# Turning the attention's scores on VectorE instead of TensorE from block 3 on, in an attention and two-MoE kernel

## Chip, cores and metric

The kernel runs on one core of a Trainium2 chip. Times are device microseconds (us) of one execution; the time of the kernel is the median of three runs.

## The reference

Three stages over 4 x 768 = 3072 tokens of width 512, all in float32. `a` is chunked attention with 8 heads, `moe` a two-layer SiLU MLP, and `moe2` a soft mixture of 8 experts with 4 slots each.

```python
for c in range(nc):                       # chunks of 32 queries
    k_ctx = k[:, :, max(0, 32*c - 16):min(S, 32*c + 40)]      # 16 keys left, 8 right
    k_full = concatenate([mem_k, k_ctx]); v_full = concatenate([mem_v, v_ctx])   # 8 more: 64 keys
    a = exp(scale * q_c @ k_full.T - max); a = a / (sum(a) + 1e-09)
    out[:, :, 32*c:32*c + 32] = a @ v_full
x = out as [3072, 512]
h = x @ w_in; x = (h * sigmoid(h)) @ w_out            # 512 -> 2048 -> 512
logits = x @ phi                                       # 32 slots
d = softmax of logits over the tokens; slot_input = d.T @ x
slot_out[e] = relu(slot_input[e] @ w1[e]) @ w2[e]
out = (softmax of logits over the slots) @ slot_out
```

## The kernel before

The tokens go through in seven blocks (256, 384, 512, 512, 512, 512, 384). Blocks 0 and 1 run in an opening whose order is written out as a string; from block 2 on two nested loops run: over the blocks j, and in each over 16 slots i, one for each 128 columns of the hidden layer.

In a slot `emit_h` (L359) issues 12 matmuls that fill one PSUM bank with 128 hidden values of the block's tokens (ps_h; x and w_in are split into a high and a low part, and three products are added). Two banks take turns, 0 and 1, so the emission of slot i+2 may begin only when slot i's bank has been read. ScalarE reads it for `g_tanh` (L379), VectorE for `g_mult` (L383), and then `g_turn` (L387) turns the result in 32x32 squares on VectorE. `logits` (L402) multiplies four slots' results with a folded w_out and phi; it stands in three slots of a block, and for the last four in slot 0 of the next.

Beside that the slots hold two kinds of other work, put in by `at(j, i, half, ...)`: half 0 comes behind the emission (and the logits), half 1 behind tanh, mult and turn of the slot. The first kind is the attention of the tokens that the next block needs, in groups of 128 tokens. A group passes through three visits of `place`, which lie three slots apart (slots 1, 5, 8, 11, 14 of block 2, slots 5, 8, 11, 14 of blocks 3 to 5):

- its scores: TensorE in half 0 (`a_scores`, L266, queries in the partitions, 8 heads x 64 keys along a row); in half 1 max (L274, L278 at the ends of a sequence) and subtraction (L287, L290) on VectorE and exp (L293) on ScalarE, and a slot later sum, inverse (L297 to L301) and the product with it (L191) on POOL
- its turn: `a_turn` (L311) makes four TensorE transposes of 128x128 with the identity into one PSUM bank, `a_keep` copies it to SBUF on ScalarE; two heads' 64 keys then lie in the partitions
- its values: `a_values` (L326), 32 matmuls with 64x64 weights from v and 64x32 scores; `a_hi` on ScalarE and `a_lo` (L343) on VectorE split the result into the high and low part of x

So one slot holds values(g), turn(g+1) and scores(g+2), in this order on TensorE. The second kind of other work is the routing of the block before (`routing`, slots 0 to 9): softmax pieces on VectorE and ScalarE, `route_slots` (L504) on TensorE, and the sums `route_acc` (L515) on VectorE. The conversion of w_out (`wo_conv`: two ScalarE instructions and L214 on VectorE) is spread over slots by the list WO.

Each engine works its queue in program order; TensorE loads weights ahead. The unnormalized scores of all groups from 5 on lie in one place (A in aarena), and so did their turned form.

Of the kernel before, what the change touches and what calls it, by code (L numbers as in the profile page):

```python
# [7 lines left out]
F32 = mybir.dt.float32  # L8
# [5 lines left out]
ALU = mybir.AluOpType  # L14
# [7 lines left out]
NG = NTOK // 128  # L22
# [30 lines left out]
def attn_moe_softmoe_kernel(  # L53
# [13 lines left out]
    nc = tc.nc  # L67
# [116 lines left out]
    def copy(eng, out, in_):  # L184
        if eng == "a":
            nc.scalar.activation(out=out, in_=in_, func=ACTF.Copy)  # L186
        else:
            nc.vector.tensor_copy(out=out, in_=in_)
# [126 lines left out]
        copy(eng, at_t[g], ps_t.pop(g))  # L315

    def a_values(g, *bs):
        AT, vt = at_t.pop(g), v_t.pop(g)
        px = ps_t[g] = [bank(b, [128, 2, 128], "ps_x") for b in bs or (None, None)]
        for c in range(4):  # L320
            q = slice(32 * c, 32 * c + 32)
            for u in range(2):
                for s, r in ((0, 0), (1, 1), (0, 1), (1, 0)):
                    k, h = slice(64 * s, 64 * s + 64), slice(64 * r, 64 * r + 64)
                    n = 2 * r + u
                    nc.tensor.matmul(px[s][h, u, q], vt[k, n, c], AT[k, n, q], start=True, stop=True)  # L326

    def x_half(x, g, s):
        o = 128 * g - tok0[blk[g]]
        t = x[blk[g]][s]  # L330
        return bass.AP(tensor=t.tensor, offset=t[:, o:o + 1].offset, ap=[t.ap[0], [BLOCKS[blk[g]], 2], [1, 128]])
# [14 lines left out]

# [234 lines left out]

    slots = {}

    def at(j, i, half, fn, *args):
        slots.setdefault((j, i, half), []).append((fn, args))


    def place(j, i, values, turn, scores, b=None):  # L590
        if values is not None:
            at(j, i, 0, a_values, values)
            at(j, i, 0, load_v, values + 1)
            at(j, i, 1, a_hi, values)
            at(j, i, 1, a_lo, values)
        if turn is not None and turn < NG:
            at(j, i, 0, a_turn, turn, b)
            at(j, i, 1, a_keep, turn, "a")
        if scores is not None and scores < NG:
            at(j, i, 0, a_scores, scores)  # L600
            at(j, i, 0, load_qk, scores + 1)
            at(j, i, 1, a_max, scores)
# [25 lines left out]
    for j in range(3, NB):  # L628
        at(j, 0, 0, logits, j - 1, f_order(j - 1)[-1] // 4)
        routing(j, 0, j - 1)  # L630
    for n, i in enumerate((1, 5, 8, 11, 14)):
        g = tok0[3] // 128 - 1 + n
        place(2, i, g if n else None, g + 1, g + 2, (None, 2, 3, 3, 3)[n])
    for j in range(3, L):
        for n, i in enumerate((5, 8, 11, 14)[:BLOCKS[j + 1] // 128]):
            g = tok0[j + 1] // 128 + n
            place(j, i, g, g + 1, g + 2, 2 + (j + 1) % 2)
    at(3, 1, 0, load_ew, *words(garena, 3072, 4096))
    at(L, 4, 1, load_ew, *words(z, NF * BLOCKS[L], 10240))
    at(3, 6, 1, wp_copies)  # L640
    WO = [(2, 15)] + [(j, i) for j in range(3, L) for i in (2, 7, 10, 13, 15)]
    for u in range(16):
        for k in range(4):
            at(*WO[u], 1, wo_conv, u, k)
# [267 lines left out]
def _layout(inputs):  # L912
    import numpy as np

    f = np.float32
    c = np.ascontiguousarray
    q, k, vv = inputs["q"], inputs["k"], inputs["v"]
    mk, mv = inputs["mem_k"], inputs["mem_v"]
    B, H, S, D = q.shape
    G = S // 128  # L920

    blocks = [0, 1, 2, 3, 4, 5, 6, 19, 7, 8, 9, 10, 19, 11, 12, 13, 14, 19, 15, 16, 17, 18]
    starts = (0, 4, 9, 14)
    keys = np.zeros((2, B, H, G, 20, 8, D), f)
    for i, (src, mem) in enumerate(((k, mk), (vv, mv))):
        for g in range(G):
            lo, hi = max(0, 128 * g - 16), min(S, 128 * g + 136)
            rows = keys[i, :, :, g].reshape(B, H, 160, D)
            rows[:, :, lo - 128 * g + 16:hi - 128 * g + 16] = src[:, :, lo:hi]
            rows[:, :, 152:160] = mem  # L930
            keys[i, :, :, g] = rows.reshape(B, H, 20, 8, D)
    kk = keys[0][:, :, :, blocks].reshape(B, 4, 2, G, 176, D)
    qk = np.zeros((2, D, B, G, 4, 304), f)
    qk[..., 0:128] = q.reshape(B, 4, 2, G, 128, D).transpose(2, 5, 0, 3, 1, 4)
    qk[..., 128:304] = kk.transpose(2, 5, 0, 3, 1, 4)

    vw = np.stack([keys[1][:, :, :, blocks[n:n + 8]].reshape(B, 2, 2, 2, G, 64, D) for n in starts], axis=5)
    vw = vw.transpose(2, 6, 0, 4, 3, 1, 5, 7)
    w_in, w_out = inputs["moe_w_in"], inputs["moe_w_out"]
    win = w_in.reshape(4, 128, 16, 128).transpose(2, 1, 0, 3)  # L940

    woutt = w_out.reshape(16, 128, 4, 128).transpose(0, 3, 2, 1)
    wout = w_out.reshape(4, 4, 4, 32, 512).transpose(2, 0, 1, 3, 4)
    phi = inputs["moe2_phi"].reshape(4, 128, 32).transpose(1, 0, 2)
    w1 = inputs["moe2_w1"].reshape(2, 4, 4, 128, 2, 512).transpose(0, 2, 4, 3, 1, 5)
    w1 = c(w1).reshape(16, 128, 2, 1024).transpose(0, 2, 1, 3)

# [40 lines left out]
```

## Time and profile before

| | us |
|---|---|
| median of three runs (482.71 to 483.04) | 482.81 |
| the profiled execution, its own time | 482.95 |
| its span on the core | 481.2 |
| TensorE busy (matmuls) | 457.8 |
| VectorE busy | 310.0 |
| ScalarE busy | 194.5 |
| POOL busy | 41.8 |

The span is what the profile covers; the time of an execution is 1.75 us longer. Busy time is the time in which an engine works on an instruction; waits of a queue are not in it. Matmuls overlap in the records, so TensorE's busy time counts each stretch once. The chain that ended last is followed back from the last instruction, at each step to what released it; an engine that fills the chain is the one that sets the end there.

### The profile page before, as it was taken

The page shows a single profiled execution, that of the slowest core. Times are in us where ns is not written, and L with a number is a line of the kernel's source. Part 1 is how long each engine was busy: PE and PEld are TensorE (multiplying, and loading weights), DVE is VectorE, ACT ScalarE, POOL GpSimd, SP SyncE. Part 2 cuts the span into 40 slices and gives each one's busy share as a digit, 9 for nine tenths or more (in the row PEclk, how much of TensorE's full clock was granted, in tenths as well). Part 3 has the DMA queues.
Part 4 walks back from the last instruction along what each step waited for, and adds up shares of the span by engine and source line. Part 5 has one row for each costly group of instructions (what it writes and reads, how often), then busy time and mean ns, then how long its engine had stood idle before and what let it go on. Part 6 is the DMA issues. An engine that isn't in the chain of part 4 may idle for free.

```text
span 481.2 us, 14612 instructions
## 1 busy us (share of the span) xinstructions
PE 457.8 (95%) x6432; PEld 346.3 (72%) x6433; DVE 310.0 (64%) x687; ACT 194.5 (40%) x403; POOL 41.8 (9%) x41
## 2 busy tenths in 40 slices
PE   5889999999999999999999999999999999999981
PEld 2789888988776777677866778766787789543641
DVE  4837787787577766677867667686755765531061
ACT  3648788863342234234443244441433222311041
POOL 0412133210000001000110000010000000000000
PEclk9559999999999999999999999999999999999996
DMA  8937688564121235123442235411133997799998
GB/s 329 378 142 265 231 288 307 172 229 142 53 57 42 97 98 184 45 97 140 142 150 80 79 108 190 143 46 49 50 125 112 389 409 273 291 412 410 407 349 276
DMA packets 29727, 93.67 MB, mean 195 GB/s; under 512 B 2784, under 2 KB 9184, under 8 KB 29664
## 3 DMA queue, kind: packets, MB, share of 16 engines
q1 hardware_dynamic: 29664, 92.74, 53.0%
q8 instruction: 50, 0.82, 0.7%
q14 instruction: 13, 0.11, 0.1%
HBM read 86.44 MB, written 6.29 MB: 193 GB/s over the span
## 4 chain that ended last, share of the span: by engine, by line
PE 89%; DMA 4%; DVE 2%; ACT 1%; issue 1%; SPq 0%; DVEq 0%; ACTq 0%
PE ps_h L359 55%; PE ps_x L326 6%; PE ps_a L504 6%; PE ps_l L402 5%; PE ps_s L266 3%; PE ps_t L311 3%; PE ps_o L825 3%; PE ps_e L793 3%; DMA oarena<-in_woutt_dram 3%; DMA oarena<-in_win_dram 1%; PE ps_f L875 1%; PE ps_q L235 1%; PE ps_in L760 1%; PE ps_sum L741 1%; PE ps_r L419 1%
## 5 line engine op out<-in xcount | busy, mean ns | idle before, releaser
L359 PE MATMUL ps_h<-x,w 128*128 128x512 f32 (+2 forms) x704 | 152.5, 361 | 1.7 <-DVE garena L383 1.4
L359 PEld LDWEIGHTS ps_h<-x,w 128*128 128x128 f32 x704 | 125.2, 190 | 22.7 <-issue 5.0
L359 PE MATMUL ps_h<-x1a,w 128*128 128x512 f32 (+2 forms) x544 | 139.4, 363 | 0.0
L383 DVE SCALAR_TENSOR_TENSOR garena<-garena,ps_h 128x512 f32<-128x512 f32 (+2 forms) x112 | 67.9, 607 | 72.0 <-ACT garena L379 71.5
L359 PEld LDWEIGHTS ps_h<-x1a,w 128*128 128x128 f32 x544 | 99.6, 189 | 20.1 <-issue 6.1
L379 ACT ACTIVATE garena<-ps_h 128x512 f32<-128x512 f32 (+2 forms) x112 | 59.8, 534 | 132.9 <-PE ps_h L359 124.0
L387 DVE STREAM_TRANSPOSE z<-garena 128x512 f32<-128x512 f32 (+2 forms) x112 | 70.1, 631 | 4.5 <-PE ps_a L504 0.9
L191 POOL TENSOR_TENSOR aarena<-aarena,smm 128x512 f32<-128x512 f32 x19 | 20.6, 1085 | 233.9 <-DVE smm L301 204.6
L214 DVE SCALAR_TENSOR_TENSOR oarena<-oarena 128x512 uint32<-128x512 uint32 x46 | 32.6, 723 | 10.6 <-ACT oarena L208 10.4
L206 ACT ACTIVATE oarena<-oarena 128x512 f32<-128x512 f32 x46 | 30.5, 668 | 18.4 <-DMA oarena<-in_win_dram 11.7
L208 ACT ACTIVATE oarena<-oarena 128x512 uint32<-128x512 uint16 x48 | 31.7, 671 | 0.0
L326 PEld LDWEIGHTS ps_x<-aarena 64*64 64x64 f32 x1280 | 21.7, 139 | 12.5 <-issue 4.0
L504 PE MATMUL ps_a<-z,d 32*32 32x512 f32 x768 | 27.0, 598 | 0.6 <-DVE d L475 0.6
L326 PE MATMUL ps_x<-aarena 64*64 64x32 f32 x1280 | 24.1, 224 | 1.2 <-issue 1.2
L359 PE MATMUL ps_h<-x1b,w 128*128 128x512 f32 x64 | 25.0, 391 | 0.0
L293 ACT ACTIVATE aarena<-aarena 128x512 f32<-128x512 f32 x20 | 12.6, 631 | 30.5 <-DVE aarena L287 15.7
L402 PE MATMUL ps_l<-garena,aarena 128*32 128x512 f32 (+2 forms) x216 | 24.7, 544 | 0.0
L274 DVE TENSOR_REDUCE mx<-ps_s 128x4 f32<-128x256 f32 x48 | 17.8, 413 | 5.8 <-PE ps_s L266 5.8
L191 POOL TENSOR_TENSOR w<-oarena,w 128x512 fp32r<-128x512 f32 x12 | 15.8, 1319 | 55.4 <-ACT w L186 55.4
L504 PEld LDWEIGHTS ps_a<-z,d 32*32 32x32 f32 x768 | 12.1, 103 | 11.7 <-issue 7.0
L515 DVE SCALAR_TENSOR_TENSOR acc<-acc,al,ps_a 128x512 f32<-128x512 f32 x20 | 13.9, 743 | 7.0 <-PE ps_a L504 7.0
L266 PE MATMUL ps_s<-aarena 64*32 64x64 f32 x1280 | 17.2, 224 | 0.7 <-DMA aarena<-in_qk_dram 0.7
(194 smaller groups left out, 432.1 us busy)
## 6 DMA issues: line engine op xcount, KB each, us to landing
aarena<-in_qk_dram SPq DMA_DIRECT2D x20, 608.0 KB, 5.4
aarena<-in_v_dram SPq DMA_DIRECT2D x20, 512.0 KB, 4.3
w<-in_w_dram SPq DMA_DIRECT2D x20, 512.0 KB, 7.1
oarena<-in_win_dram SPq DMA_DIRECT2D x16, 512.0 KB, 5.6
oarena<-in_woutt_dram SPq DMA_DIRECT2D x16, 512.0 KB, 6.0
oarena<-in_wout_dram SPq DMA_DIRECT2D x16, 512.0 KB, 3.2
z<-in_w_dram SPq DMA_DIRECT2D x10, 512.0 KB, 7.8
oarena<-in_w_dram SPq DMA_DIRECT2D x9, 512.0 KB, 10.2
```

The costliest lines, as they stand in the source:

```text
L191: (nc.gpsimd if eng == "p" else nc.vector).tensor_tensor(**kw)
L206: nc.scalar.activation(out=x, in_=hi_w.bitcast(F32), func=ACTF.Prelu, scale=REBIAS, alpha=-(2.0**32))
L208: nc.scalar.activation(out=lo_w, in_=raw.bitcast(U16)[:, :, 1], func=ACTF.Copy, scale=2.0**-13, bias=-4095.75 / 8192)
L214: nc.vector.scalar_tensor_tensor(out=xb, in0=xb, scalar=3, in1=lo_w, op0=ALU.logical_shift_left, op1=ALU.bitwise_or)
L266: nc.tensor.matmul(ps[r][q, p], t[h, p, q], t[h, p, w:w + 64], start=True, stop=True)
L326: nc.tensor.matmul(px[s][h, u, q], vt[k, n, c], AT[k, n, q], start=True, stop=True)
L359: nc.tensor.matmul(ph, w_t[f][:, wi, 128 * c:128 * c + 128], x[c], start=(c == 0 and m == 0), stop=(c == 3 and m == 2),)
L379: nc.scalar.activation(out=g_tile(j, f), in_=h_t[j, f], func=ACTF.Tanh, scale=0.5)
L383: nc.vector.scalar_tensor_tensor(out=g, in0=g, scalar=1.0, in1=h_t.pop((j, f)), op0=ALU.add, op1=ALU.mult)
L387: nc.vector.transpose(out=z_view(j)[:, slot], in_=g_t[j, f])
L402: nc.tensor.matmul(rt[j, "pl"][32 * m:32 * m + 32], wp[:, f], g_t[j, f], start=(k == ks[0]), stop=(k == ks[-1] or j == L and m > 1 and k = ...
L504: nc.tensor.matmul(ps[q][32 * cg:32 * cg + 32], d[p, t], zv[p, :, t], start=(b < 4), stop=(b >= nb - 4), tile_position=(32 * q, 32 * cg),)
```

## The change

For groups 9 to 23 (the tokens of blocks 3 to 6) `a_turn` and `a_keep` are gone. `v_turn` takes their place on VectorE: one instruction turns all of A, 128 partitions by 512, in 32x32 squares, which puts the first or second 32 keys of each of the four chunks into the chunk's own 32 partitions; four instructions of 32 partitions by 256 turn the other 32 keys of a chunk and write them to the neighbouring 32 partitions, so that a chunk's 64 keys lie in 64 partitions. The turned form alternates between two places (aarena, oarena). `a_values_turned` takes 32 matmuls of the same shape as before; the heads' results lie in another order, so v is laid out differently for these groups on the host (same size), and `a_hi` and `a_lo` write 64 tokens of four head pairs instead of 128 tokens of two. Where x's four parts lie in two buffers, `a_lo` takes two instructions for each half instead of one; that is so for the low part of block 4.

The turn of group g+1 moves to half 1 of the slot in front of values(g): in slots 0, 4, 7, 10, 13 of block 2, and 3, 7, 10, 13 of blocks 3 to 5, there ahead of the other work in slot 3. The conversions of w_out move from slots 7, 10, 13 to 6, 9, 12.

```diff
+    FIRST_TURNED = tok0[3] // 128
+    def v_turn(g):
+        A = a_t.pop(g).rearrange("p h (a k) -> p h a k", a=2)
+        o = aarena[:, 2752:3264] if g % 2 else oarena[:, 6656:7168]
+        AT = at_t[g] = o.rearrange("p (h a q) -> p h a q", h=8, a=2)
+        nc.vector.transpose(out=o, in_=A.rearrange("p h a k -> p (h a k)"))
+        for c in range(4):
+            a = c % 2
+            i, k = slice(32 * c, 32 * c + 32), slice(32 * (c ^ 1), 32 * (c ^ 1) + 32)
+            nc.vector.transpose(out=AT[k, :, a], in_=A[i, :, 1 - a])
+    def a_values_turned(g):
...
+        px = ps_t[g] = [bank(None, [128, 4, 64], "ps_x") for _ in range(2)]
+        for a in range(2):
+            for p in range(4):
+                for s, r in ((0, 0), (1, 1), (0, 1), (1, 0)):
+                    k, h = slice(64 * s, 64 * s + 64), slice(64 * r, 64 * r + 64)
+                    nc.tensor.matmul(
+                        px[s][h, 2 * (p % 2) + p // 2, 32 * a:32 * a + 32], vt[k, 4 * r + p, a], AT[k, 4 * r + p, a],
+                        start=True, stop=True,
+                    )
...
+    def x_pieces(xs, g):
+        if g < FIRST_TURNED:
+            return [(0, 2)]
+        x = xs[blk[g]]
+        return [(0, 4)] if x[0].tensor.name == x[3].tensor.name else [(0, 2), (2, 2)]
...
-        if turn is not None and turn < NG:
-            at(j, i, 0, a_turn, turn, b)
-            at(j, i, 1, a_keep, turn, "a")
...
+    TURNS = {2: (0, 4, 7, 10, 13)}
     for n, i in enumerate((1, 5, 8, 11, 14)):
         g = tok0[3] // 128 - 1 + n
-        place(2, i, g if n else None, g + 1, g + 2, (None, 2, 3, 3, 3)[n])
+        at(2, TURNS[2][n], 1, v_turn, g + 1)
+        place(2, i, g if n else None, g + 2)
...
-            place(j, i, g, g + 1, g + 2, 2 + (j + 1) % 2)
+            if g + 1 < NG:
+                at(j, i - 1 if n else 3, 1, v_turn, g + 1, first=(n == 0))
+            place(j, i, g, g + 2)
...
-    WO = [(2, 15)] + [(j, i) for j in range(3, L) for i in (2, 7, 10, 13, 15)]
+    WO = [(2, 15)] + [(j, i) for j in range(3, L) for i in (2, 6, 9, 12, 15)]
```

VectorE's queue in block 2, from the mult of slot 7 (ps_h) to the low part of x in slot 8 (x<-ps_x), before; acc is the routing's sum, cm and call its softmax:

```order
L383 SCALAR_TENSOR_TENSOR garena<-garena,ps_h 128x512
L387 STREAM_TRANSPOSE z<-garena 128x512
L523 TENSOR_REDUCE cm<-call 128x2
L524 TENSOR_TENSOR call<-call,cm 128x64
L515 SCALAR_TENSOR_TENSOR acc<-acc,al,ps_a 128x512 x4
L383 SCALAR_TENSOR_TENSOR garena<-garena,ps_h 128x512
L387 STREAM_TRANSPOSE z<-garena 128x512
L490 SCALAR_TENSOR_TENSOR s_run<-s_run,al,sb 128x1
L343 TENSOR_TENSOR x_71<-ps_x,x_71 128x2x128 x2
```

The same place now:

```order
L423 SCALAR_TENSOR_TENSOR garena<-garena,ps_h 128x512
L427 STREAM_TRANSPOSE z<-garena 128x512
L563 TENSOR_REDUCE cm<-call 128x2
L564 TENSOR_TENSOR call<-call,cm 128x64
L555 SCALAR_TENSOR_TENSOR acc<-acc,al,ps_a 128x512 x4
L339 STREAM_TRANSPOSE aarena<-aarena 128x512
L343 STREAM_TRANSPOSE aarena<-aarena 32x8x32 x4
L423 SCALAR_TENSOR_TENSOR garena<-garena,ps_h 128x512
L427 STREAM_TRANSPOSE z<-garena 128x512
L530 SCALAR_TENSOR_TENSOR s_run<-s_run,al,sb 128x1
L382 TENSOR_TENSOR x_71<-ps_x,x_71 128x4x64 x2
```

The five turns of group 11 (L339, L343) stand between the sums of slot 7 and the mult of slot 8.

TensorE's queue in block 3, from the emission of slot 6 over values, turn and scores of slot 8 to that of slot 9, before (x_71 is x, the w's are the slots' weights):

```order
L359 MATMUL ps_h<-x_71,w_648 128x512 x12
L359 MATMUL ps_h<-x_71,w_702 128x512 x12
L359 MATMUL ps_h<-x_71,w_751 128x512 x12
...
L326 MATMUL ps_x<-aarena 64x32 x32
L311 MATMUL ps_t<-cst,aarena 128x128 x4
L266 MATMUL ps_s<-aarena 32x64 x32
L359 MATMUL ps_h<-x_71,w_804 128x512 x12
```

The same place now:

```order
L399 MATMUL ps_h<-x_71,w_648 128x512 x12
L399 MATMUL ps_h<-x_71,w_702 128x512 x12
L399 MATMUL ps_h<-x_71,w_751 128x512 x12
...
L352 MATMUL ps_x<-oarena,aarena 64x32 x32
L266 MATMUL ps_s<-aarena 32x64 x32
L399 MATMUL ps_h<-x_71,w_804 128x512 x12
```

The row of the four transposes (L311) is gone between values and scores, and the values read the turned scores of an even group from oarena.

## Rows read from the trace of the kernel before

**Rows 1.** The page, parts 1 and 4: busy time, and the chain's shares

```profile
PE 457.8 (95%) x6432; PEld 346.3 (72%) x6433; DVE 310.0 (64%) x687; ACT 194.5 (40%) x403; POOL 41.8 (9%) x41
...
PE 89%; DMA 4%; DVE 2%; ACT 1%; issue 1%; SPq 0%; DVEq 0%; ACTq 0%
```

**Rows 2.** The chain in order of time, block 3: start, us, what

```profile
218.32 1.00 PE ps_l L402 x8
219.31 1.06 PE ps_x L326 x64
220.38 0.59 PE ps_t L311 x4
...
221.75 8.38 PE ps_h L359 x36
```

**Rows 3.** Busy by stretch, block 3: length, then PE, PEld, DVE, ACT, POOL, clock

```profile
186.60:250.10 63.50, 63.50 (x886) 47.25 (x890) 45.90 (x99) 24.30 (x48) 4.43 (x4) 1.00 0.36 124
```

**Rows 4.** Timeline of VectorE, slots 9 to 12 of block 3: start, us, instruction [idle before]

```profile
225.37 0.69 DVE L383 SCALAR_TENSOR_TENSOR garena<-garena,ps_h 128x512 f32<-128x512 f32 x1 [1.62 <-ACT garena L379]
226.09 0.71 DVE L387 STREAM_TRANSPOSE z<-garena 128x512 f32<-128x512 f32 x1
226.72 0.25 DVE L531 TENSOR_REDUCE cs<-call 128x4 f32<-128x128 f32 x1
...
227.63 0.68 DVE L297 TENSOR_REDUCE smm<-aarena 128x8 f32<-128x512 f32 x1
...
228.67 0.64 DVE L383 SCALAR_TENSOR_TENSOR garena<-garena,ps_h 128x512 f32<-128x512 f32 x1
...
229.97 0.65 DVE L214 SCALAR_TENSOR_TENSOR oarena<-oarena 128x512 uint32<-128x512 uint32 x1
...
232.16 0.38 DVE L343 TENSOR_TENSOR x1a<-ps_x,x1a 128x256 fp32r<-128x256 f32 x1
...
232.80 0.74 DVE L274 TENSOR_REDUCE mx<-ps_s 128x4 f32<-128x256 f32 x2
233.57 0.71 DVE L278 TENSOR_REDUCE mx<-ps_s 32x4 f32<-32x224 f32 x2
234.31 0.76 DVE L287 TENSOR_TENSOR aarena<-ps_s,mx 128x256 f32<-128x256 f32 x2
...
236.50 0.69 DVE L383 SCALAR_TENSOR_TENSOR garena<-garena,ps_h 128x512 f32<-128x512 f32 x1 [1.24 <-ACT garena L379]
```

**Rows 5.** Groups by line and shape: count | busy us, mean ns | idle before

```profile
L387 DVE STREAM_TRANSPOSE z<-garena 128x512 f32<-128x512 f32 x64 | 45.2, 709 | 3.2 <-PE ps_a L504 0.9
...
L387 DVE STREAM_TRANSPOSE z<-garena 128x256 f32<-128x256 f32 x16 | 6.5, 429 | 0.3
...
L482 DVE STREAM_TRANSPOSE call<-ps_r 32x128 f32<-32x128 f32 x16 | 4.8, 302 | 0.2
```

**Rows 6.** Timeline of VectorE, four turns of 32 partitions in block 4

```profile
259.23 1.25 DVE L482 STREAM_TRANSPOSE call<-ps_r 32x128 f32<-32x128 f32 x4
```

**Rows 7.** Timeline of ScalarE, exp behind the subtraction of slot 11, block 3

```profile
235.35 0.63 ACT L293 ACTIVATE aarena<-aarena 128x512 f32<-128x512 f32 x1 [2.86 <-DVE aarena L290]
```

**Rows 8.** Timeline of VectorE, block 2, slots 4 to 7

```profile
139.53 0.56 DVE L449 TENSOR_REDUCE nm<-ps_r 128x1 f32<-128x384 f32 x1 [0.96 <-PE ps_r L419]
...
146.34 0.69 DVE L383 SCALAR_TENSOR_TENSOR garena<-garena,ps_h 128x512 f32<-128x512 f32 x1 [1.24 <-ACT garena L379]
...
151.70 2.71 DVE L515 SCALAR_TENSOR_TENSOR acc<-acc,al,ps_a 128x512 f32<-128x512 f32 x4
```

**Rows 9.** The chain in order of time, block 2: emission of slot 8

```profile
150.93 2.98 PE ps_h L359 x12
```

**Rows 10.** Timeline of POOL, block 3: the product of slot 9

```profile
228.92 1.04 POOL L191 TENSOR_TENSOR aarena<-aarena,smm 128x512 f32<-128x512 f32 x1 [11.72 <-DVE smm L301]
```

**Rows 11.** Busy by stretch, opening: columns as in rows 3

```profile
9.00:12.00 3.00, 0.00 (x0) 0.00 (x0) 2.75 (x9) 2.24 (x4) 0.40 (x1) 0.98 1.02 415
12.00:18.00 6.00, 5.00 (x146) 4.15 (x147) 5.52 (x17) 3.34 (x6) 2.73 (x3) 0.50 1.02 407
```

More of the change, by code (lines that the diff above doesn't have):

```diff
@@ L317, in a_values @@
     def a_values(g, *bs):
+        if g >= FIRST_TURNED:
+            return a_values_turned(g)
         AT, vt = at_t.pop(g), v_t.pop(g)
@@ L326, in a_values, with x_piece @@
                     nc.tensor.matmul(px[s][h, u, q], vt[k, n, c], AT[k, n, q], start=True, stop=True)
[L328 to L331, printed above, removed]
+    FIRST_TURNED = tok0[3] // 128
[9 more added lines that the diff above has]
+    def a_values_turned(g):
+        AT, vt = at_t.pop(g), v_t.pop(g).rearrange("p a b c -> p (a b c)").rearrange("p (h a e) -> p h a e", h=8, a=2)
+        px = ps_t[g] = [bank(None, [128, 4, 64], "ps_x") for _ in range(2)]
[7 more added lines that the diff above has]
+                    )
+    def x_piece(xs, g, s, i, m):
+        o, n = 128 * g - tok0[blk[g]], BLOCKS[blk[g]]
+        x, w = (xs[blk[g]][s], 128) if g < FIRST_TURNED else (xs[blk[g]][(0, 2, 1, 3)[i]], 64)
+        o += 0 if g < FIRST_TURNED else 64 * s
+        return bass.AP(tensor=x.tensor, offset=x[:, o:o + 1].offset, ap=[x.ap[0], [n, m], [1, w]])
+    def x_pieces(xs, g):
[3 more added lines that the diff above has]
+        return [(0, 4)] if x[0].tensor.name == x[3].tensor.name else [(0, 2), (2, 2)]
     def a_hi(g):
@@ L337, in a_hi @@
         for s in range(2):
-            copy("a", x_half(xh_t, g, s), ps_t[g][s])
+            for i, m in x_pieces(xh_t, g):
+                copy("a", x_piece(xh_t, g, s, i, m), ps_t[g][s][:, i:i + m])
     def a_lo(g):
@@ L342, in a_lo @@
         for s in range(2):
-            nc.vector.tensor_tensor(
-                out=x_half(xl_t, g, s), in0=px[s], in1=x_half(xh_t, g, s).bitcast(F32), op=ALU.subtract
-            )
+            for i, m in x_pieces(xl_t, g):
+                nc.vector.tensor_tensor(
+                    out=x_piece(xl_t, g, s, i, m), in0=px[s][:, i:i + m],
+                    in1=x_piece(xh_t, g, s, i, m).bitcast(F32), op=ALU.subtract,
+                )
     h_t, g_t = {}, {}
@@ L584, in attn_moe_softmoe_kernel, with at, place @@
     slots = {}
-    def at(j, i, half, fn, *args):
-        slots.setdefault((j, i, half), []).append((fn, args))
-    def place(j, i, values, turn, scores, b=None):
+    def at(j, i, half, fn, *args, first=False):
+        work = slots.setdefault((j, i, half), [])
+        work.insert(0 if first else len(work), (fn, args))
+    def place(j, i, values, scores):
         if values is not None:
@@ L595, in place @@
             at(j, i, 1, a_lo, values)
-        if turn is not None and turn < NG:
-            at(j, i, 0, a_turn, turn, b)
-            at(j, i, 1, a_keep, turn, "a")
-        if scores is not None and scores < NG:
+        if scores < NG:
             at(j, i, 0, a_scores, scores)
@@ L937, in _layout @@
     vw = np.stack([keys[1][:, :, :, blocks[n:n + 8]].reshape(B, 2, 2, 2, G, 64, D) for n in starts], axis=5)
-    vw = vw.transpose(2, 6, 0, 4, 3, 1, 5, 7)
+    v0 = vw.transpose(2, 6, 0, 4, 3, 1, 5, 7).reshape(128, B * G, 1024)
+    v1 = vw.reshape(B, 2, 2, 2, G, 2, 2, 64, D).transpose(5, 7, 0, 4, 3, 1, 2, 6, 8).reshape(128, B * G, 1024)
+    vw = np.concatenate([v0[:, 0:9], v1[:, 9:]], axis=1)
     w_in, w_out = inputs["moe_w_in"], inputs["moe_w_out"]
```

## Prediction, made before the changed kernel ran

> **What bounds the kernel now.** I read the page's busy shares first, then the chain that ended last, the chain in order of time inside one block, and last VectorE's timeline in the same stretch. TensorE is busy 457.8 of 481.2 us and makes 89% of the chain [rows 1]. Inside block 3 the chain is nothing but TensorE, piece behind piece: logits 1.00, values (ps_x) 1.06, the turn of the scores (ps_t) 0.59, scores, then three emissions of ps_h in 8.38, 2.79 each [rows 2]. So a TensorE microsecond taken out there is a microsecond of the end, as long as nobody makes TensorE wait. VectorE is busy 45.90 of the 63.50 us of block 3 [rows 3], 72%. That share is an average and hides the loop that matters: TensorE has two ps_h banks, so emission i+2 may start only when g_mult of slot i (L383) has read its bank, and VectorE works its queue strictly in order. The reader should see in VectorE's rows that from the mult at 225.37 to the subtraction at 234.31 one instruction follows the other [rows 4]: round slot 11 the queue is full already.
>
> **What comes off.** Fifteen groups of 128 tokens (9 to 23) lose four TensorE transposes. The ps_t piece is 0.59 us in the chain wherever it stands between values and scores [rows 2], so 15 x 0.59 = 8.85 us. The values stay 32 matmuls of 64x32 from the same four corners of the array, so their 1.06 stays; scores stay. ScalarE loses 15 copies; it is no bound (busy 24.30 of 63.50 [rows 3]) and I cost that at nothing: what it waits for is VectorE. The moved weight conversions keep their number; v is loaded in the same size, and SP's queue is unchanged.
>
> **What comes on.** VectorE gets 15 times a 128x512 turn and four of 32x256. The first has a price: 0.709 [rows 5]. The second has none in the trace. A 32x128 turn took 0.302, and 256 more elements cost 0.709 - 0.429 = 0.280 [rows 5], so 128 more cost 0.140: I take 0.442. Four of 32x128 in a row took 1.25 [rows 6], that is 4 x 0.302 and 0.04: they follow one another without overlap, while a 128x512 turn of 0.71 lets the next instruction begin after 0.63 [rows 4]. So one group costs 0.71 + 0.04 + 4 x 0.442 + 0.04 = 2.56 us of VectorE's queue. The bounds of the small turn are 0.302 (half the elements) and 0.709 (the whole 128x512 tile); 0.442 lies nearest to the 32-row rows and the 128x256 row's 0.429.
> [...]
>
> **The walk.** One round is three slots, from g_mult of the slot behind a group's scores to the same place one group later. VectorE's round after the change, from block 3 [rows 4]: three times g_mult and its turn 1.35 (225.37 to 226.72) = 4.05; sum and inverse 1.04 (227.63 to 228.67); a weight conversion 0.65; the new turns 2.56; two low parts 0.64; max 0.70; subtraction 0.75; and a wait of 1.24. The wait is a loop: exp (ScalarE, behind the subtraction [rows 7]) stands in ScalarE's queue ahead of the next tanh, and g_mult needs that tanh; row 236.50 shows it whenever VectorE is late. Sum 11.6. TensorE's round is 3 x 2.79 + 1.06 + 0.79 (the 2.44 from 219.31 to 221.75 without 0.59) + 1.00 where logits stand: 11.2, or 10.2 without [rows 2]. So VectorE's loop is the longer one and TensorE waits as soon as its slack is used up. The slack at the start: g_mult(9) ended at 226.06 and emission 11 began at 221.75 + 2 x 2.79 = 227.33, so 1.27 [rows 2, 4].
> Block 3 also splits the low parts into four (x lies in two buffers there); half the elements each, so between 0 and 0.5 more, I take 0.25. Slots 5 to 8: 11.6 + 0.25 + 0.55 (two softmax instructions like the one at 226.72) = 12.4 against 11.2 uses 1.2 of the slack. Slots 8 to 11: + 0.91 softmax (226.72 to 227.63) + 0.25 + 0.85 sequence edge (233.57, and the clearing behind 234.31) = 13.6 against 10.2: 3.4 us of waiting before emissions 13 and 14. Slots 11 to 14: 11.6 + 0.25 + 0.8 against 11.2: 1.4 more, at block 4's first logits. Block 3: 4.8.
> Block 4, without split and without edges: 12.2 against 11.2, 12.5 against 10.2, 11.6 against 11.2: 1.0 + 2.3 - 1.27 = 2.0, and 0.4. Block 4: 2.4. Block 5 has turns in slots 3 and 7 only, and its slack carries them: nothing.
> Block 2 has no conversions (round 11.0) but two routings. The turn of slot 4 meets 0.96 of idle time (139.53) and 0.59 of earlier TensorE, so g_mult(6) comes 1.0 later, ending at 148.0 instead of 147.03; emission 8 comes 2 x 0.59 earlier, 149.75 instead of 150.93 [rows 8, 9]: slack 1.7. Slots 5 to 8 add routing to VectorE: four 32-row turns 1.1 (a little under the 1.25 of [rows 6], with fewer elements), softmax 0.35, the accumulation 2.71 [rows 8], 0.1, an edge 0.75: 16.0 against 11.3 of TensorE gives 4.7 - 1.7 = 3.0 of waiting at emissions 10 and 11. Then softmax and a wait for ScalarE, 1.7 together: 12.7 against 11.3, 1.4; then 11.8 against 11.3, 0.5. Block 2: 4.9.
> **Sum**: -8.85 + 4.9 + 4.8 + 2.4 = +3.3 us. The profiled execution took 482.95 (span 481.2), 0.14 over the median of 482.81; 482.95 + 3.3 is 486.2, on the median's scale **486.1**.
> SP and POOL: the new turn waits on VectorE's queue for POOL's product; that starts behind the inverse and takes 1.04 (228.92 to 229.96 [rows 10]), while the turn of slot 10 comes no sooner than 230.0, now with a conversion ahead of it. I cost it at nothing; if it were late, every g_mult behind it would be too.
>
> **Rivals.**
> First, the turns are short: at 0.302 a group costs 0.71 + 0.04 + 4 x 0.302 + 0.04 = 2.0, and with each start 0.08 early, as after the 128x512 turn of 0.71 [rows 4], 2.1. Then block 2 waits 1.9 + 0.8, block 3 3.1 and block 4 0.9: 6.7 in all, -2.1, **480.7**. For it: no row shows a 32-row turn of 256 elements, nor one that changes partitions. Against: at 128 partitions 256 more elements cost 0.280 [rows 5]. [...]
> Second, it cancels: a group at 2.2 to 2.4, or queues with half a microsecond more give at each long wait: **482.9**.
> [...]
> That the change doesn't do what it says would be ps_t rows left in blocks 2 to 5; the order shows none, so it gets no chance.
>
> **How the numbers follow.** Forecast 0.51 (its own range 484 to 488.5), short turns 0.21, cancelling 0.13, clock 0.15. Both signs hold much, so the range goes from the short turns' 480.7 to 490.0, the clock's time with some more of unknown price; at the far bound of 0.709 per turn the walk would give 497, which I leave out. 0.2%, about 1 us, is what a measurement here can tell: faster 0.21, within it 0.13, slower 0.66.
>
> **What would show it.** Right: the 32x256 turn at 0.42 to 0.46; TensorE idle some 12 us in blocks 2 to 4 in front of ps_h, released by VectorE's g_mult, most in slots 10, 11 and 14 of block 2 and 13, 14 of block 3; nothing in block 5; ps_x at 1.06. Wrong: a small turn near 0.3; idle time of TensorE under 9 us; g_mult late without TensorE waiting; or waits in front of ps_x.

## The result, and the profile after

The changed kernel takes **487.44 us** (median of 4 runs, 486.26 to 487.71) against 482.93 of the kernel before on the same chip: a ratio of 1.0086, 95% interval 1.0066 to 1.0106. The forecast was 486.1, slower. The profiled execution took 487.32 us, its span is 485.5; line numbers up to L311 are those of before, those behind it are 2 to 43 higher (values L352, emissions L399, g_tanh L419, g_mult L423, g_turn L427, logits L442, accumulation L555; the new turns are L339 and L343).

The page of the changed kernel, parts 1 and 4, to be held against [rows 1]:

```profile
PE 451.4 (93%) x6373; PEld 340.0 (70%) x6373; DVE 344.1 (71%) x770; ACT 185.0 (38%) x388; POOL 43.8 (9%) x41
...
PE 69%; DVE 18%; DMA 5%; ACT 3%; issue 2%; SPq 1%; DVEq 0%; ACTq 0%
```

TensorE lost 6.4 us of work, VectorE gained 34.1, and the end came 4.4 us later. The second line tells why: VectorE's share of the chain that ended last went from 2% to 18%. In block 3 that chain, which was TensorE from end to end in [rows 2], now reads so (start, us, what):

```profile
219.54 0.63 DVE aarena L339
220.19 0.43 DVE aarena L343
...
222.01 0.70 DVE garena L423
...
226.79 0.70 DVE garena L423
...
238.16 0.77 DVE aarena L287 x2
239.20 0.63 ACT aarena L293
239.82 0.49 ACT garena L419
240.34 0.70 DVE garena L423
241.09 4.50 PE ps_h L399 x12
```

From 214.1 to 241.1 us none of the chain's pieces is TensorE's: the new turns, the mults, the softmax's subtraction, ScalarE's exp and tanh follow one another, and TensorE comes in again only with the emission at 241.09. The waits of TensorE in blocks 2 to 5 (what waited, for whom: us in all, times, longest):

```profile
PE ps_h L399 <- DVE garena L423: 6.7, 4, 2.8
PE ps_x L352 <- DVE acc L555: 1.7, 1, 1.7
PE ps_h L399 <- issue: 1.1, 1, 1.1
```

and where they stand in TensorE's timeline, the wait in brackets:

```profile
155.00 1.14 PE L352 MATMUL ps_x<-oarena,aarena 64*64 64x32 f32 x64 [1.65 <-DVE acc L555]
...
163.70 0.50 PE L399 MATMUL ps_h<-x1a,w 128*128 128x512 f32 x1 [1.10 <-DVE garena L423]
...
176.53 0.50 PE L399 MATMUL ps_h<-x1a,w 128*128 128x512 f32 x1 [1.30 <-DVE garena L423]
...
241.09 4.50 PE L399 MATMUL ps_h<-x,w 128*128 128x512 f32 x12 [2.78 <-DVE garena L423]
...
278.42 0.85 PE L399 MATMUL ps_h<-x1a,w 128*128 128x512 f32 x3 [1.12 <-issue]
...
306.85 1.19 PE L399 MATMUL ps_h<-x1a,w 128*128 128x512 f32 x4 [1.53 <-DVE garena L423]
```

Three of them stand in block 2, one in block 3, two in block 4, none in block 5. The busy time by block (length, then PE, PEld, DVE, ACT, POOL, granted clock, DMA share, GB/s) shows how little a share of busy time tells: VectorE holds TensorE up with 57.91 of 68.72 us busy in block 2, 84%.

```profile
119.27:187.99 68.72, 64.66 (x973) 46.68 (x972) 57.91 (x138) 19.46 (x44) 4.18 (x4) 1.00 0.23 78
187.99:254.01 66.02, 63.24 (x867) 46.67 (x866) 56.14 (x128) 22.41 (x46) 5.31 (x4) 0.97 0.35 119
254.01:318.31 64.30, 61.65 (x868) 45.51 (x867) 52.93 (x113) 21.18 (x43) 5.31 (x4) 1.00 0.33 114
318.31:375.48 57.17, 57.17 (x611) 42.34 (x610) 43.77 (x87) 19.63 (x39) 2.65 (x2) 1.00 0.21 72
```

These stretches run from a block's first logits to the next block's. The opening ahead of them differs by up to 3 us between the profiled executions of the kernels below, so the lengths of the blocks are compared, not the times of day:

| block | before | after | forecast for after | e1 | e2 | e3 | e5 | e6 | e7 | e8 | e9 |
|---|---|---|---|---|---|---|---|---|---|---|---|
| 2 | 66.71 | 68.72 | 68.66 | 64.20 | 69.75 | 64.80 | 68.72 | 68.72 | 64.83 | 68.72 | 64.84 |
| 3 | 63.48 | 66.02 | 65.92 | 61.50 | 65.18 | 62.24 | 65.02 | 64.60 | 61.29 | 66.15 | 61.30 |
| 4 | 63.49 | 64.30 | 63.53 | 62.78 | 64.29 | 62.44 | 65.74 | 63.90 | 62.55 | 63.05 | 61.18 |
| 5 | 58.06 | 57.17 | 56.88 | 57.17 | 58.06 | 57.18 | 57.18 | 57.17 | 57.38 | 57.18 | 57.33 |

(The forecast's column is the length before, less 0.59 for each group of the block, five, four, four and two, plus the block's forecast waits 4.9, 4.8, 2.4 and 0. e4, not in the table, keeps the lengths of before within 0.03.)

### The profile page after: what moved, and what is told of

It is laid out like the page before. It is cut to its first block, busy times and chain, and to the rows that moved or that the text cites. A ratio compares the mean times of both kernels' runs of the same rounds, so it can differ in the third digit from the quotient of the medians.

```text
span 485.5 us, 14527 instructions
## 1 busy us (share of the span) xinstructions
PE 451.4 (93%) x6373; PEld 340.0 (70%) x6373; DVE 344.1 (71%) x770; ACT 185.0 (38%) x388; POOL 43.8 (9%) x41
## 4 chain that ended last, share of the span: by engine, by line
PE 69%; DVE 18%; DMA 5%; ACT 3%; issue 2%; SPq 1%; DVEq 0%; ACTq 0%
PE ps_h L399 41%; PE ps_a L544 5%; PE ps_l L442 4%; DVE garena L423 3%; PE ps_o L868 3%; DVE z L427 3%; PE ps_e L836 3%; PE ps_x L328 3%; DMA oarena<-in_woutt_dram 2%; DMA oarena<-in_win_dram 2%; PE ps_s L266 2%; PE ps_x L352 2%; DVE oarena L343 1%; PE ps_f L918 1%; ACT garena L419 1%
## 5 line engine op out<-in xcount | busy, mean ns | idle before, releaser
L399 PE MATMUL ps_h<-x,w 128*128 128x512 f32 (+2 forms) x704 | 154.3, 364 | 4.5 <-DVE garena L423 3.9
L399 PE MATMUL ps_h<-x1a,w 128*128 128x512 f32 (+2 forms) x544 | 140.7, 364 | 5.1 <-DVE garena L423 3.9
L399 PEld LDWEIGHTS ps_h<-x,w 128*128 128x128 f32 x704 | 126.3, 192 | 25.8 <-DVE garena L423 5.3
L399 PEld LDWEIGHTS ps_h<-x1a,w 128*128 128x128 f32 x544 | 99.6, 189 | 26.8 <-issue 7.7
L423 DVE SCALAR_TENSOR_TENSOR garena<-garena,ps_h 128x512 f32<-128x512 f32 (+2 forms) x112 | 68.0, 607 | 56.6 <-ACT garena L419 55.7
L419 ACT ACTIVATE garena<-ps_h 128x512 f32<-128x512 f32 (+2 forms) x112 | 59.3, 532 | 121.4 <-PE ps_h L399 109.3
L427 DVE STREAM_TRANSPOSE z<-garena 128x512 f32<-128x512 f32 (+2 forms) x112 | 70.1, 631 | 4.0 <-PE ps_a L544 0.4
L191 POOL TENSOR_TENSOR aarena<-aarena,smm 128x512 f32<-128x512 f32 x19 | 22.7, 1194 | 237.2 <-DVE smm L301 213.9
L214 DVE SCALAR_TENSOR_TENSOR oarena<-oarena 128x512 uint32<-128x512 uint32 x46 | 32.5, 720 | 5.3 <-ACT oarena L208 5.2
L399 PE MATMUL ps_h<-x1b,w 128*128 128x512 f32 x64 | 25.0, 391 | 0.0
L442 PE MATMUL ps_l<-garena,aarena 128*32 128x512 f32 (+2 forms) x216 | 25.0, 543 | 0.0
L544 PEld LDWEIGHTS ps_a<-z,d 32*32 32x32 f32 x768 | 12.1, 103 | 11.7 <-issue 7.0
L555 DVE SCALAR_TENSOR_TENSOR acc<-acc,al,ps_a 128x512 f32<-128x512 f32 x20 | 13.9, 742 | 2.5 <-PE ps_a L544 2.4
L266 PEld LDWEIGHTS ps_s<-aarena 64*32 64x32 f32 x1280 | 13.9, 105 | 2.1 <-DMA aarena<-in_qk_dram 0.8
L287 DVE TENSOR_TENSOR aarena<-ps_s,mx 128x256 f32<-128x256 f32 x40 | 14.8, 410 | 0.1
```

What stands on the lines that cost most here:

```text
L191: (nc.gpsimd if eng == "p" else nc.vector).tensor_tensor(**kw)
L214: nc.vector.scalar_tensor_tensor(out=xb, in0=xb, scalar=3, in1=lo_w, op0=ALU.logical_shift_left, op1=ALU.bitwise_or)
L266: nc.tensor.matmul(ps[r][q, p], t[h, p, q], t[h, p, w:w + 64], start=True, stop=True)
L399: nc.tensor.matmul(ph, w_t[f][:, wi, 128 * c:128 * c + 128], x[c], start=(c == 0 and m == 0), stop=(c == 3 and m == 2),)
L419: nc.scalar.activation(out=g_tile(j, f), in_=h_t[j, f], func=ACTF.Tanh, scale=0.5)
L423: nc.vector.scalar_tensor_tensor(out=g, in0=g, scalar=1.0, in1=h_t.pop((j, f)), op0=ALU.add, op1=ALU.mult)
```

## The experiments

**The theory**: the turn of a group costs VectorE 2.5 us in a loop of VectorE and ScalarE that was nearly as long as TensorE's round; it became the longer one, and TensorE waits for its banks. **Rivals**: the delay comes from something else in the change (the values read from another place, the moved conversions), or from TensorE's clock.

### e1: without the four small turns

```
 def v_turn(g):
     nc.vector.transpose(out=o, in_=A.rearrange(...))
-    for c in range(4):
-        a = c % 2
-        i, k = slice(32 * c, 32 * c + 32), slice(32 * (c ^ 1), 32 * (c ^ 1) + 32)
-        nc.vector.transpose(out=AT[k, :, a], in_=A[i, :, 1 - a])
```

> The changed kernel without the four 32-row turns of each group; the crossing halves of the scores are left out, so it shows the time alone. Theory (VectorE's queue holds TensorE): a group costs 0.74 of the queue instead of 2.53, the rounds of VectorE are shorter than TensorE's again but for two of them, TensorE's waits fall from some 10 us to under 1 and nearly the whole 8.85 us come out: 474.5 to 475.5. Rival (the new values, their banks or the moved conversions hold TensorE): the waits stay, 484 to 487. Rival (the clock alone): the waits stay but under 2.8 us each, about 485.

Measured: 477.38 us (473.78 to 478.6), ratio to before 0.9888 (0.9843 to 0.9933). TensorE's waits in blocks 2 to 5:

```profile
PE ps_h L395 <- issue: 1.5, 1, 1.5
PE ps_x L348 <- DVE acc L551: 0.2, 1, 0.2
```

No emission waits for a mult any more. Blocks 2 to 5 are 6.1 us shorter than before (251.74 to 245.65), of 8.85 that could come off; 1.5 of the rest is a gap that nothing in the trace releases (see e8), 0.2 the wait for the accumulation, and 1.1 stands in no wait. The 1.8 us of small turns in each group are the whole difference between a gain and a loss: everything else in the change is in this kernel.

### e2: the kernel before, with the new turns on top

```
+def v_extra(g):                      # o = oarena[:, 6656:7168], read by nobody
+    nc.vector.transpose(out=o, in_=A.rearrange(...))
+    for c in range(4):
+        ...
+        nc.vector.transpose(out=AT[k, :, a], in_=A[i, :, 1 - a])
...
+at(2, (0, 4, 7, 10, 13)[n], 1, v_extra, g + 1)
+at(j, i - 1 if n else 3, 1, v_extra, g + 1, first=(n == 0))
...
-WO = [(2, 15)] + [(j, i) for j in range(3, L) for i in (2, 7, 10, 13, 15)]
+WO = [(2, 15)] + [(j, i) for j in range(3, L) for i in (2, 6, 9, 12, 15)]
```

> The kernel before, with TensorE's turns, their copies and the old values as they were, and the five turns of each group added on VectorE into a place that nobody reads, at the changed kernel's slots; the conversions at the changed kernel's slots too. Theory: the same queue of VectorE holds TensorE, whose rounds are 0.59 longer here, so less: 4 to 6 us of waits in blocks 2 to 4, 487 to 489. Rival (the new values or their banks cost the time): no waits, 483.

Measured: 488.5 us (488.08 to 488.88), 1.0131 (1.0107 to 1.0154).

```profile
PE ps_h L369 <- DVE garena L393: 4.3, 4, 1.7
```

TensorE's own work and everything it reads are those of before; VectorE has more to do, the conversions stand in the changed kernel's slots (e5 tries that part), and blocks 2 to 4 get 3.0, 1.7 and 0.8 us longer. So a VectorE queue that is longer by one group's turns is enough to delay the end. The change then has 8.85 us of TensorE to set against that, but a shorter round of TensorE only makes it wait longer (8.4 us for VectorE in the changed kernel, 4.3 here): the changed kernel is 1.1 us better than this one, not 8.85.

### e3: exp behind the next tanh, in the changed kernel; e4: the same in the kernel before

```
-at(j, i, 1, a_exp, scores)
+at(j, i + 1, 1, a_exp, scores)
```

e3 takes the wait of 1.24 us out of VectorE's round, by the order of two ScalarE instructions alone, and leaves all of the turns in.

> The changed kernel, with exp issued a slot later, behind the next slot's tanh in ScalarE's queue. Theory (VectorE's round is its work plus the wait of 1.24 for exp and tanh): the wait goes, VectorE's round falls from 11.6 to some 10.4 and below TensorE's, and 7 to 8 of the 8.85 us come out: 475 to 477. Rival (VectorE's work alone is the bound, at 82 to 86% busy): 1 to 3 us better, 484 to 486. Rival (values or banks): no change, 487.

> The kernel before, with exp a slot later as in e3. Theory: TensorE is never held in blocks 2 to 5 here, so nothing changes, 482.9 within 0.5. Rival (the later exp is a gain by itself, through ScalarE or the start of a block): 480 to 482.

Measured: e3 479.12 us (475.38 to 481.39), 0.9928 (0.9894 to 0.9962), and e4 482.54, 0.9995 (0.9972 to 1.0017). ScalarE's rows ahead of the mult of slot 9 in block 2, first of the changed kernel:

```profile
161.81 0.63 ACT L293 ACTIVATE aarena<-aarena 128x512 f32<-128x512 f32 x1 [4.96 <-DVE aarena L290]
162.35 1.07 ACT L419 ACTIVATE garena<-ps_h 128x512 f32<-128x512 f32 x2
```

then of e3:

```profile
159.98 0.60 ACT L419 ACTIVATE garena<-ps_h 128x512 f32<-128x512 f32 x1 [3.05 <-PE ps_h L399]
161.88 0.63 ACT L293 ACTIVATE aarena<-aarena 128x512 f32<-128x512 f32 x1 [1.31 <-DVE aarena L290]
```

and VectorE's mult that needs the tanh, in e3:

```profile
160.81 0.73 DVE L287 TENSOR_TENSOR aarena<-ps_s,mx 128x256 f32<-128x256 f32 x2
161.62 0.17 DVE L290 MEMSET aarena<- 32x128 f32 x1
161.72 0.62 DVE L423 SCALAR_TENSOR_TENSOR garena<-garena,ps_h 128x512 f32<-128x512 f32 x1
```

In e3 the tanh starts as soon as its emission is done, at 159.98, and the mult follows VectorE's clearing with nothing between. In the changed kernel, whose VectorE is at the same place at the same time (the subtraction at 160.74), ScalarE sits idle up to 161.81 because exp, ahead of the tanh, waits for VectorE; the tanh starts at 162.35, and the mult waits 1.24 for it and starts at 162.96 instead of 161.72. With 1.24 us off each of the rounds, VectorE's loop of 11.6 falls, by the prediction's sum, to 10.4, under TensorE's 11.2; measured, blocks 2 to 5 fall from 256.21 to 246.66. e3 is faster than both kernels; e4 shows that the same order is worth nothing where VectorE isn't late. The medians of e1 and e3 both lie 2 us above the ranges expected. Their profiled executions, 478.6 us (the longest of e1's four) and 479.01, say where: the opening took 1.3 and 0.7 longer than before (last logits of block 1 at 121.07 and 120.52, 119.82 before), the gap in block 4 took 1.5 and 1.1, and in e3 0.52 was left before the values of group 10 and 0.78 before an emission of block 3.

### e5: the moved weight conversions back in their old slots

```
-WO = [(2, 15)] + [(j, i) for j in range(3, L) for i in (2, 6, 9, 12, 15)]
+WO = [(2, 15)] + [(j, i) for j in range(3, L) for i in (2, 7, 10, 13, 15)]
```

> The changed kernel with the conversions of w_out back in slots 7, 10 and 13, ahead of the new turns' next mult. Theory (VectorE's round is the bound): a round keeps its length, only the place of 0.65 us moves behind the new turns, so 0.5 to 1.5 us more than the changed kernel: 487.5 to 489. Rival (the moved conversions are what holds TensorE): 483 to 485.

Measured: 487.39 us (487.0 to 489.96), 1.01 (1.0067 to 1.0133): no different from the changed kernel, and just under the 487.5 to 489 that were expected. The rival's 483 to 485 falls: the moved conversions are not what holds TensorE. But the trace has the half microsecond that was expected: in block 3 the emission of slot 14 begins 53.54 us behind the block's first logits, in the changed kernel 53.10. TensorE's clock, which did not fall behind that wait in e5, gave back about as much (see e6).

### e6: work for TensorE in the long wait of block 3

```
+at(3, 13, 0, keep_warm, 8, 2)
```

In the changed kernel the clock fell behind the 2.78 us wait at 241.09, the emission there taking 4.50 instead of 2.79 (busy by stretch; PE is the second number, the granted clock the third from the end):

```profile
238.00:240.00 2.00, 0.30 (x2) 0.00 (x0) 1.00 (x4) 0.80 (x2) 0.00 (x0) 1.00 0.00 0
240.00:242.00 2.00, 0.92 (x2) 0.82 (x3) 1.62 (x3) 1.90 (x4) 0.00 (x0) 0.72 0.00 0
242.00:244.00 2.00, 2.00 (x6) 1.54 (x6) 1.90 (x6) 0.00 (x0) 1.07 (x1) 0.50 0.00 0
```

> The changed kernel with eight 128x512 bf16 matmuls into an unused bank (some 1.7 us of TensorE) behind the emission of slot 13 of block 3, where TensorE waited 2.78 us and the granted clock fell. If the clock's fall is a cost of its own, the filler lies inside the wait, the emission of slot 14 takes 2.8 instead of 4.5 us and the kernel is 1 to 2 us faster: 485.5 to 486.5. Rival (VectorE alone sets that place, a fast TensorE only waits more behind it): within 0.5 of the changed kernel, 487.0 to 487.9.

Measured: 486.33 us (486.27 to 486.73), 1.0069 (1.0047 to 1.009), 1.1 less than the changed kernel and inside the range that was expected if the fall costs. The blocks bear that out only in part. In e6 the clock stayed at 1.00 in block 3, and the emission of slot 14 took 3.01:

```profile
241.87 3.01 PE L399 MATMUL ps_h<-x,w 128*128 128x512 f32 x12 [1.04 <-DVE garena L423]
```

Blocks 3 and 4 together are 128.50 against 130.32. 1.1 of these 1.8 is the gap in block 4 that nothing releases: it isn't there in e6. The other 0.7 is what was left of the fall; e8, which has the fall and neither the gap nor the filler, has 129.20. The fall had made the emission 1.5 us longer, but a TensorE that comes 1.5 sooner meets VectorE late again: the next logits took 1.93 in e6 where those of the changed kernel took 1.06, and inside them the weight load of the seventh logit waits for the mult of slot 15:

```profile
254.21 0.14 PEld L442 LDWEIGHTS ps_l<-garena,aarena 128*32 128x32 f32 x2 [0.73 <-DVE garena L423]
```

So 0.87 of the 1.5 would have been waited anyway. The rest still stands where the routing in block 4 begins on TensorE, first in e6, then in the changed kernel:

```profile
264.03 4.46 PE L544 MATMUL ps_a<-z,d 32*32 32x512 f32 x128
263.86 4.46 PE L544 MATMUL ps_a<-z,d 32*32 32x512 f32 x128
```

Counted from block 3's first logits (188.73 and 187.99) that is 75.30 us in e6 and 75.87 in the changed kernel. **e5** has the same wait of 2.78 at the same place, and there the clock stayed up too (same columns):

```profile
242.00:244.00 2.00, 2.00 (x10) 1.36 (x8) 1.90 (x6) 0.00 (x0) 1.05 (x1) 1.00 0.00 0
```

Its emission of slot 14 took 3.04, not 4.50, and its next logits again 1.93:

```profile
252.53 1.93 PE L442 MATMUL ps_l<-garena,aarena 128*32 128x512 f32 x8
```

Counted alike, it began that emission 0.44 later than the changed kernel, and the routing in block 4 0.14 sooner (75.73): again some 0.6. In block 4, where its conversions stand in other slots as well, it loses more than that (65.74 us against 64.30), so its time doesn't show it.

Block 2 is the other case. In e6 the clock fell there, behind a wait of 1.66 us, and block 2 is 68.72 long all the same (more under e8). A fall costs what the next waits don't take back: nothing in block 2, some 0.6 us in block 3.

### e7: the routing's softmax earlier, on top of e3

```
-at(j, i + 7, 1, route_c, b)
-at(j, i + 9, 1, route_cn, b)
+at(j, i + (4 if b > 1 else 7), 1, route_c, b)
+at(j, i + (5 if b > 1 else 9), 1, route_cn, b)
```

> e3 (exp a slot later) with the routing's softmax pieces of blocks 2 to 5, 0.5 and 0.9 us of VectorE, taken from slots 7 and 9 of the next block to its slots 4 and 5, where VectorE has idle time. Theory: the shortest round of TensorE (slots 8 to 11) meets 0.9 us less of VectorE's, the wait of 0.78 before emission 14 of block 3 goes: 0.5 to 1.2 us faster than e3, 478 to 478.6. Rival (what is left of e3's loss is not VectorE's queue): as e3, 479.1.

Measured: 478.49 us (477.41 to 479.98), 0.9906 (0.9872 to 0.9941).

```profile
PE ps_h L399 <- issue: 1.2, 1, 1.2
PE ps_x L352 <- DVE acc L555: 0.5, 1, 0.5
```

The last wait on a mult is gone; block 3 is 61.29 long, 63.48 less 4 x 0.59 being 61.12. The step from e3 is 0.6 us, and the intervals of the two overlap.

### e8 and e9: TensorE's instruction stream eight matmuls longer

The gap at 278.42 has no releaser, stands at the emission of slot 6 in block 4, and is found in every kernel whose TensorE stream is that of the changed kernel (after, e1, e3, e5, e7: 1.1 to 1.5 us); before, e2 and e4 don't have it, nor has e6, with eight matmuls more ahead of it. So the same number of matmuls, short ones, went into the idle time at the start, of the changed kernel (e8) and of e7 (e9):

```
-keep_warm(10)
+keep_warm(10, short=8)     # eight more, of 64 columns
```

> The changed kernel with eight more short matmuls (64 columns) in the warm-up at its start, in idle time; everything behind them on TensorE stands eight matmuls later in its instruction stream. Theory (the 1.1 us of TensorE's idle time at the emission of slot 6 in block 4, which nothing in the trace releases, belongs to a place in the instruction stream, as in the run with the filler, where it was gone): the gap at 278 is gone or at another place; if gone, the rest of block 4 is some 0.4 to 1.1 shorter and the time 486.3 to 487. Rival (the gap belongs to the program's place, where the loads of the next keys start): the gap stays, 487.4. The waits on g_mult and on the accumulation stay as they are, 8.4 us in all, unless TensorE's clock falls behind one of them; then the next wait gets shorter by about what the slow emission lost.

> The kernel with the late exp and the early softmax, with the same eight short matmuls in the warm-up. There TensorE's waits in blocks 2 to 5 are down to 0.5 before the values of slot 10 in block 2 and the 1.2 us of block 4 that nothing releases. Theory (a place in the instruction stream): the gap goes or moves; if it goes, the time is 477.3, 1.2 less than 478.5. Rival (the place where the next keys' loads start): the gap stays at slot 6 of block 4 and the time is 478.5.

Measured: e8 488.43 us (485.63 to 489.66), 1.0091 (1.0057 to 1.0124); e9 478.05 us (475.7 to 479.18), 0.9877 (0.9848 to 0.9905). In this comparison the kernel before itself spread from 479.3 to 486.4, so neither differs measurably from its partner. e8's median lies above the 486.3 to 487 that were expected: in its profiled execution blocks 2 to 5 took 1.1 us less than in the changed kernel (255.10 against 256.21), but the opening 2.3 more (it ends at 121.56, there at 119.27). The traces decide more: the gap is gone from blocks 2 to 5 in both. (In its opening e8 has a stop of 1.31 us without a releaser, at 77.86, where the changed kernel has one of 0.61.) TensorE's waits in blocks 2 to 5 of e8, and of e9:

```profile
PE ps_h L401 <- DVE garena L425: 5.4, 3, 2.8
PE ps_x L354 <- DVE acc L557: 1.7, 1, 1.7
```

```profile
PE ps_x L354 <- DVE acc L557: 0.5, 1, 0.5
```

Block 4 of e9 is 1.4 shorter than that of e7, block 4 of e8 1.25 shorter than that of the changed kernel. The place where the next keys' loads start is the same in all of them, so that rival falls; in these runs the gap goes with a place in TensorE's instructions. What TensorE does there isn't shown.

e8 also has the clock's fall twice, behind the waits of block 2 and of block 3. Busy by stretch in block 2:

```profile
158.00:160.00 2.00, 2.00 (x98) 1.77 (x91) 1.93 (x5) 0.66 (x2) 0.00 (x0) 0.81 0.31 47
160.00:162.00 2.00, 2.00 (x6) 1.52 (x6) 1.97 (x6) 0.00 (x0) 0.00 (x0) 0.50 0.86 321
```

The next emission that waits in the changed kernel, at 163.70 for 1.10 us, doesn't wait here, and block 2 is 68.72 in e8 and e6, where the clock fell in it, and 68.72 in the changed kernel and e5, where it didn't.

## Why the prediction was right, and where its steps were off

**What bounds the kernel** held. TensorE, piece behind piece, was the chain of before, and VectorE's queue becomes it; e2 and e1 show that from both sides. One reading was a little off: VectorE's queue round slot 11 was not quite without a break, since ahead of the mult at 230.81, which [rows 4] leave out, it waited 0.18 us for tanh.

**What comes off**: block 5, which the walk left without waits, got 0.89 shorter of the 1.18 forecast, and block 3 of e7 and e9, with nearly no wait left, comes within 0.2 of the forecast 61.12. The whole of the 8.85 did not come off: e9, with 0.5 us of waits left, has blocks 2 to 5 shorter by 7.1 (251.74 to 244.65), so the term was some 1.3 too large, and no run shows why. Scores stayed at 0.79 and values at 1.06 to 1.11. No matmul of the changed kernel in blocks 2 to 5 waits for ScalarE (the three rows of TensorE's waits name VectorE twice, 6.7 and 1.7 us, and nobody for the 1.1), as the copies' price of nothing has it.

**What comes on**: the price that no row showed was right. The groups by line and shape (count | busy us, mean ns | idle before):

```profile
L343 DVE STREAM_TRANSPOSE aarena<-aarena 32x256 f32<-32x256 f32 x32 | 14.0, 436 | 0.6
...
L339 DVE STREAM_TRANSPOSE aarena<-aarena 128x512 f32<-128x512 f32 x8 | 5.6, 695 | 0.0
```

and one group in VectorE's timeline:

```profile
137.52 0.70 DVE L339 STREAM_TRANSPOSE oarena<-aarena 128x512 f32<-128x512 f32 x1
138.25 1.79 DVE L343 STREAM_TRANSPOSE oarena<-aarena 32x256 f32<-32x256 f32 x4
140.06 0.56 DVE L489 TENSOR_REDUCE nm<-ps_r 128x1 f32<-128x384 f32 x1
```

From 137.52 to 140.06 are 2.54 us, 2.56 were forecast; a small turn takes 0.436 for 0.442, and four of them 1.79, one behind the other, as read from the four 32x128 turns of [rows 6]. In these rows the price goes with the row length and not with the number of partitions: 0.436 for 32x256 and 0.429 for 128x256, 0.302 for 32x128 and 0.709 for 128x512 [rows 5].

**The walk** came out closer than its pieces had reason to. Its long round in block 2, forecast at 16.0, is seen between the mults that wait for ScalarE:

```profile
146.87 0.69 DVE L423 SCALAR_TENSOR_TENSOR garena<-garena,ps_h 128x512 f32<-128x512 f32 x1 [1.24 <-ACT garena L419]
...
162.96 0.69 DVE L423 SCALAR_TENSOR_TENSOR garena<-garena,ps_h 128x512 f32<-128x512 f32 x1 [1.24 <-ACT garena L419]
```

16.09 us, and the wait is the 1.24 of [rows 4]. In block 3 the round from the mult at 226.79 to that at 240.34 in the chain above is 13.55, forecast 13.6. The block lengths in the table follow: block 2 within 0.1, blocks 3 and 4 together 130.32 against 129.45, and 129.2 without the 1.12 us gap.

That the total came out within 1.4 us is partly luck. Blocks 2 to 5 got 4.5 us longer, so 13.3 were lost against the 8.85; the walk had 12.1, all of them waits for VectorE. Of the 13.3, 8.4 are TensorE's waits for VectorE, 1.1 is the gap in block 4, 1.5 the slow emission, and the other 2.3 are small pieces, with the part of the 8.85 that did not come off among them.

Four points were off:

- **Where block 2's wait stands.** The prediction put 3.0 us before emissions 10 and 11 and named waits in front of ps_x as a sign of error. 1.65 of it stands in front of group 10's values, ahead of emission 9, since they need a bank that the accumulation (L555, 152.24 to 154.95) still reads; 1.10 stands before emission 11. The sum is 2.75. The walk hadn't followed this bank, though its slack could be read: by [rows 8] the accumulation ended at 154.41, and by [rows 2, 9] the values began at 150.93 + 2.98 + 1.00 = 154.91. The time is the same, since what TensorE waits at the one meeting with a late VectorE it needn't wait at the next.
- **The clock.** The chance of 0.15 and the range's far end of 490.0 stand for falls of the granted clock; no run shows a fall that costs that much, 3.9 us above the forecast. What the runs showed in its place: the clock fell to 0.50 in the changed kernel and in e6 once and in e8 twice, for some 3 us each time, where [rows 11] have it there for six. In block 3 of the changed kernel the fall made the emission 1.5 us longer, and 0.9 of that was given back, since TensorE came later and did not wait at the next logits (1.06, against 1.93 in e5 and e6); in block 2 of e8 and e6 all of it was, and the wait of 1.10 at 163.70 was gone. Some 0.6 of the measured time is left of it.
- **The signs.** TensorE was to be idle some 12 us in front of ps_h, and is idle 9.5 us, 6.7 of them there. Only 8.4 of the 9.5 are waits for VectorE, which is under the 9 us that were named as a sign of being wrong; a part of what is missing is the slow emission, 4.50 instead of 3.01, which counts as busy. In block 3 the wait is 2.78, at emission 14 alone, not 3.4 at 13 and 14, and the 1.4 at block 4's first logits is seen as 0.87 (1.93 less 1.06) only where the clock stayed up, in e5 and e6.
- **The gap in block 4**, 1.12 us: in no row of before and in no term. The profiled execution came out 1.1 us over the 486.2 of the sum; the opening's 0.55 less and the tail's 0.4 more nearly cancel.

The first rival (short turns, 480.7) falls by the 0.436. The second (it cancels, 482.9) would have wanted half a microsecond more give at each long wait; e3, with 1.24 us of it in each round, shows how steep that is: 8.3 us better, and a gain over the kernel before. A version that beats both is thus e3's order, at 479.1 us; the 478.5 and 478.05 of e7 and e9, with their small additions, are within the noise of it.

## What to carry to other kernels

Before moving work to an engine that is "72% busy", walk its queue through one round of the engine it feeds and compare the two rounds, idle time that is forced by a third engine included: here 2.5 us a round went into a slack of 1.3, and blocks 2 to 5 came out 4.5 us longer, though TensorE had been spared more than 7 us of work. Look in that round for a wait that only an order makes, such as an instruction that depends on the late engine and stands in a third engine's queue ahead of one that the late engine needs; one line that changed this order was worth more than the loss. And price a slowdown of an engine that waits for another by what its next waits don't take back: a fall of the clock cost nothing in block 2 and some 0.6 of 1.5 us in block 3, and the gap in block 4, where TensorE wasn't waiting, cost its full 1.1.

## What the runs showed of the hardware that was not expected

- The same wait of 2.78 us, at the same place, was followed by a granted clock of 0.50 for some 3 us in the changed kernel and in e8, and by none in e5; a wait of 1.7 by one in e6 and e8 and by none in the changed kernel and e5. What decides between them is open.
- TensorE stood still for 1.1 to 1.5 us in block 4 at a place that goes with its instruction stream: eight matmuls more ahead of it, and the gap was gone, in three kernels of three.
- POOL's normalisation (the 128x512 product of [rows 10]) took 1194 ns in the mean in the changed kernel, 1193 in e1 and 1180 in e2, and 1085 before. It isn't the turns: e5, which has all of them and the conversions of w_out in their old slots, has 1091 (1.05, 1.04 and 1.05 us for its three products from 216 to 244 us, where the changed kernel has 1.33 each). A single product takes 1.33 us where VectorE's conversion (L214, from 230.08 to 230.73 in the changed kernel) runs beside it, and 1.04 to 1.05 where it doesn't. First the changed kernel, then e5:

```profile
230.31 1.33 POOL L191 TENSOR_TENSOR aarena<-aarena,smm 128x512 f32<-128x512 f32 x1 [11.71 <-DVE smm L301]
230.25 1.04 POOL L191 TENSOR_TENSOR aarena<-aarena,smm 128x512 f32<-128x512 f32 x1 [12.39 <-DVE smm L301]
```

The same is seen before, in the product at 250.64, which took 1.30 with a conversion beside it (250.39 to 251.04). It stayed hidden: the product at 230.31 ends at 231.64, and the turn that needs it begins at 232.00.
